# Holding back weight loads behind two joined PVs, in a one-core kernel of window attention plus gated MLP

## The chip, the cores and the metric

The kernel runs on one core of one Trainium2 chip. The metric is device time in microseconds of one execution, inputs and outputs in HBM. A core has five engines with instruction streams of their own: TensorE (PE; its weight loads are listed apart as PEld), VectorE (DVE), ScalarE (ACT), GpSimd (POOL) and SyncE (SP). They wait for each other through semaphores. Transfers are issued as instructions of an engine's stream, here nearly all of SP's, which works strictly in order: what stands behind a waiting issue waits too.

## The reference

```
xn  = layernorm(x)                                  # x: 2048 x 576, bf16
qkv = xn @ wqkv                                     # 32 heads of 18
A   = softmax(q k^T / sqrt(18), causal, window 256) v @ wo
B   = (silu(xn @ w1) * (xn @ w3)) @ w2              # 576 -> 4608 -> 576
out = x + A + B
```

## The kernel before

**Chunks.** The 2048 tokens are worked in four chunks of 512 (loop `for c in range(NC)`, line 941; chunks 0 to 3). A chunk has a projection part (q, k, v), then 36 units (line 1025), then a part called p2. In one unit 128 columns of gate and 128 of up are computed for 512 tokens: nine rounds (`for n in range(9)`, line 1033) of two matmuls that use one half of PE's rows each (`unit_pairs`, line 713), then tanh on ScalarE (722) and two multiplications on VectorE (728, 731) that leave one tile of hT. In p2 (`p2_list`, line 736) hT is multiplied by W2 (773) and the attention's output by wo (779, 699), half of the 576 output columns after the other; the residual is added (786) and the result stored (788).

**Attention between the units.** A planner counts a clock in rounds and inserts score steps (matmuls in 587, exponentials on ScalarE in 596, masks on GpSimd in 623) between rounds. Heads are grouped in four; the product of probabilities and values is a PV (644), four a chunk. PV 0 comes after a set unit (`FIRST`), PVs 1 and 2 are joined at one place (`JOINT`, line 938: unit 26 before round 6 in chunk 0, unit 27 before round 7 in chunk 1, unit 24 before round 4 in chunk 2, unit 27 before round 8 in chunk 3), PV 3 stands after unit 35. What follows a PV is spread over the next units (`later`): transposes out of PSUM (653), reciprocals (658), scaling on GpSimd (659), transposes (666), and four copies into oT issued by SP (`o_pack`, 670). For the joined PVs the first four copies are issued two units after, the other four five units after.

**Weights of gate and up.** They come in 9 column blocks a chunk, one for four units, each in six pieces of 192 KB (`load_part`, line 311). Three buffers hold blocks in turn. After every fourth unit (u = 3, 7, ... 27; line 1070) six pieces are owed, and `owe_part` issues one after rounds 3 and 8 of each following unit (line 1067), on SP, behind the matmul of that round. So the block owed after unit 23 is that of units 32 to 35, and the one owed after unit 27 is the first of the next chunk. Chunk 3 owes none after unit 27.

**W2.** Its 18 tiles a chunk (288 KB each, `load_w2`, line 342) pass through four buffers, which also hold probabilities earlier in the chunk. The first four tiles of a chunk are loaded during the units: after units 27 to 30 in chunk 0, else after units JOINT + 1, + 3, + 5 and + 7 (line 1118). In p2 each tile serves 16 matmuls, and the next tile of its buffer is loaded after them (line 777).

**The next chunk's LayerNorm.** Four tiles of 128 tokens, three of them during the units: for tile t, statistics (357 to 367) at unit JOINT - 13 + 4t, the normalizing (394) two units later, and the transposing DMA into xnT (419) three units later (`near`, line 944). Tile 3 has units 34 and 35 and a place in p2.

**Order on SP.** It is the program's order. Around the joined PVs these meet: weight pieces, transposing DMAs, W2 tiles, oT copies, and four loads of x for the residual (line 1121, after unit 29).

Of the kernel before, what the change touches and what calls it, by code (L numbers as in the profile page):

```python
# [164 lines left out]
def bass_parallel_sum__sliding_block__glu_gated_swiglu__prompt_kernel(  # L165
# [32 lines left out]
    with ExitStack() as es:  # L198
# [48 lines left out]
        def pt_keys(sl):  # L247
            kind, n = sl
            if kind in ("pt", "w2", "od"):
                return [(kind, n)]  # L250
            if kind == "sh":
                return [("sh", 2 * n), ("sh", 2 * n + 1)]
            return [("h", NF - 8 + 2 * n), ("h", NF - 7 + 2 * n)]
# [21 lines left out]
        def job():  # L275
            nonlocal job_ctr
            i = job_ctr % 3
            job_ctr += 1
            return JOBS[i]
# [14 lines left out]
        def load_x(t, eng="sp"):  # L294
            nonlocal xp_ctr
            s = xp_ctr % NXP
            xp_ctr += 1
            add(eng, lambda e: e.dma_start(xp[s][:], x2[t * 128:(t + 1) * 128, :]), w=[("xp", s)], dma=f"xp{s}")
            return s
# [638 lines left out]
        JOINT = {0: (26, 6), 1: (27, 7), 2: (24, 4), 3: (27, 8)}  # L938
        AHEAD = [40, 24, 40, 24]

        for c in range(NC):
            NS = len(steps_of(c))
            att = [(g, s) for g in range(G) for s in range(NS)]
            near = {t: tuple(JOINT[c][0] - 13 + 4 * t + k for k in (0, 2, 3)) for t in range(3)} | {3: (34, 35, 40)}
            plan = near if c + 1 < NC else {}
            stat, apply, xt = ({v[k]: i for i, v in plan.items()} for k in range(3))
            loads = {8: (2,), 17: (3,)} if c + 1 < NC else {}
# [22 lines left out]
            def later(u, what):  # L970
                side.setdefault(u, []).append(what)

            def release(j, kept):
                for g in (2 * j, 2 * j + 1):
                    for st in range(NS):
                        sl = pt_of[(c, g, st)]
                        ok = ("pt", "sh", "h", "w2") if j == 0 else ("pt", "sh")
                        if sl[0] in ok:
                            (kept if kept is not None and len(kept) < 2 and sl[0] in ("pt", "sh") else free).append(sl)
# [45 lines left out]
            for u in range(NF):  # L1025
                at_u = u
                if c == 0 and u == 0:
                    owed += 12
                if u in loads:
                    for i in loads[u]:  # L1030
                        xslot[(c + 1) * TB + i] = load_x((c + 1) * TB + i)
                b0 = jobs[u] = job()
                for n in range(9):
                    into = nxt - (clock + 9 - n)
                    if (u, n) == JOINT[c]:
                        ja = 1
                        assert next_pv == ja and ja + 1 in pv_ready and clock >= pv_ready[ja + 1], (c, next_pv, clock, pv_ready)
                        two = [job(), job()]
                        job_ctr += 1
                        kept = []  # L1040
                        _DEBUG.setdefault("joint", []).append((c, u, n, done, round(clock - pv_ready[ja + 1], 1), len([o for o in P.ops if o.eng == "pe"])))
                        for m, j in enumerate((ja, ja + 1)):
                            pv(c, j, two[m])
                            clock += PV_COST
                            release(j, kept)
                        next_pv = ja + 2
                        for m, sl in enumerate(kept):
                            uqs[2 + m:] = [pt_slot(sl).rearrange("p q r -> p (q r)").bitcast(dt.float32)]
                            uq_keys[2 + m:] = [pt_keys(sl)]
                        pv_out(two[0][0], 0)  # L1050
                        pv_out(two[0][1], 1)
                        o_scale(0)
                        pv_out(two[1][0], 2)
                        pv_out(two[1][1], 3)
                        g = 2 * ja
                        later(u, lambda g=g: (o_turn(g, 0), o_turn(g, 1), o_scale(1)))
                        later(u + 1, lambda g=g: o_turn(g + 1, 0))
                        later(u + 2, lambda g=g, ja=ja: (o_turn(g + 1, 1), o_pack(ja, "sp"), o_scale(2)))
                        later(u + 3, lambda g=g: (o_turn(g + 2, 0), o_turn(g + 2, 1), o_scale(3)))
                        later(u + 3, lambda kept=kept: free.extend(kept))  # L1060
                        later(u + 4, lambda g=g: o_turn(g + 3, 0))
                        later(u + 5, lambda g=g, ja=ja: (o_turn(g + 3, 1), o_pack(ja + 1, "sp")))
                    if (c == 0 or u or n > 1) and done < len(att) and (free or done < len(early) or done in held) and (clock >= nxt or (n == 8 and into < 3 and clock >= soon)):
                        spaced_step()
                    op = unit_pairs(c, u, n, n + 1, b0[0])
                    clock += 1
                    if n in (3, 8) or (n == 6 and c == 0 and u < 4):
                        owe_part(op)
                unit_tanh(u, b0[0])
                if u % 4 == 3 and u < NF - 8 and (c or u != 15):  # L1070
                    owed += 6
                if u == FIRST[c]:
                    j = next_pv
                    assert j == 0 and clock >= pv_ready[0], (c, clock, pv_ready)
                    next_pv += 1
                    banks = job()
                    pv(c, j, banks)
                    clock += PV_COST
                    release(j, None)
                    later(u, lambda b=banks: (pv_out(b[0], 0), pv_out(b[1], 1), o_scale(0)))  # L1080
                    later(u + 1, lambda j=j: (o_turn(2 * j, 0), o_turn(2 * j, 1), o_scale(1)))
                    later(u + 2, lambda j=j: o_turn(2 * j + 1, 0))
                    later(u + 3, lambda j=j: (o_turn(2 * j + 1, 1), o_pack(j, "sp")))
                    if j == 0:
                        for n in range(7):
                            later(u + 4 + (n if c == 0 else n // 2 + n // 6), lambda n=n: o_rest(n, "sp" if c else "act"))
                unit_h(u, b0[0])
                for what in side.pop(u, []):
                    what()
                if u in stat:  # L1090
                    t = (c + 1) * TB + stat[u]
                    for part in range(2):
                        ln_stats(t, xslot[t], part)
                if u in xt:
                    xn_send((c + 1) * TB + xt[u])
                if u in apply:
                    t = (c + 1) * TB + apply[u]
                    ln_apply(t, xslot[t])
                if c == 0 and u == 1:
                    span_main(2, G, "act", slice(2, None))  # L1100
                if c == 0 and u == 2:
                    span_last(2, G, slice(0, 1))
                if c == 0 and u in (4, 5):
                    span_last(2, G, slice(1, 3) if u == 4 else slice(3, None))
                if c == 0 and u == 13:
                    for t in range(4):
                        a0 = (4 + 14 * (t // 2)) * Dh
                        rows = A_wo[a0:a0 + 14 * Dh, :].rearrange("(s p d) f -> p s d f", p=2, d=Dh)[t % 2, :, :, :]
                        add("sp", lambda e, t=t, rows=rows: e.dma_start(wo[0:126, t, :], rows),
                            dma="wo", **{"j" if t else "w": ["wo"]})  # L1110
                if c == 0 and u == 22:
                    head = A_wo[0:4 * Dh, :]
                    add("sp", lambda e: e.dma_start(wo[126:128, 0:4, :], head.rearrange("(t d) f -> d t f", d=Dh)[16:Dh, :, :]),
                        j=["wo"], dma="wo")
                    for r in range(2):
                        add("sp", lambda e, r=r: e.dma_start(
                            wo[64 * r:64 * r + 64, 4, :], head.rearrange("(t d) f -> t d f", d=Dh)[:, 0:16, :]), j=["wo"], dma="wo")
                if u in (range(27, 31) if c == 0 else range(JOINT[c][0] + 1, JOINT[c][0] + 8, 2)):
                    load_w2(c * 2 * NFC + 4)
                if u == 29:  # L1120
                    xs = [load_x(c * TB + tt) for tt in range(TB)]
# [11 lines left out]
            for n, item in enumerate(p2_list(c)):  # L1133
# [20 lines left out]
                elif n in (100, 120) and c + 2 < NC:  # L1154
                    t = (c + 2) * TB + (n == 120)
# [32 lines left out]
```

## Time and profile before

| what | us |
|---|---|
| median of 3 runs | 558.45 |
| lowest, highest | 558.35, 559.97 |
| the profiled execution | 559.28 |
| its span (first to last instruction) | 557.5 |
| PE busy | 552.9 |
| VectorE busy | 311.2 |
| ScalarE busy | 260.3 |
| GpSimd busy | 161.9 |

The span is what the trace covers; the rest of an execution's time lies around it. All times in the views are microseconds from the span's start. In rows of groups the columns are: line, engine, operation, written and read tiles, shape and count, then busy time and mean ns of one, then idle time of the engine just before them and what ended it. In rows of a timeline: start, length, line, operation and tiles, count; neighbouring instructions of one kind are merged. In rows of DMA issues: tiles, queue, count, size of one, median time from issue to landing. In rows of waits: who waited for whom, then total, times, longest. Tiles of both weight kinds are called `w` there; L322 is a gate/up piece, L349 a W2 tile.

### The profile page before, as it was taken

To read this page: it belongs to the slowest core of one execution; us is meant where nothing else is said; L and a number is where in the kernel's file an instruction comes from. 1 tells how busy PE (TensorE), PEld (TensorE's weight loads), DVE (VectorE), ACT (ScalarE), POOL (GpSimd) and SP (SyncE) were. 2 spreads that over 40 slices of the span, in tenths; PEclk is the share of its full clock that TensorE was granted. 3 is DMA by queue.
4 is the path that set the end of the run, shared out by engine and by line. 5 is a ranking of instruction groups with operands and counts; after the bars stand their busy time and mean duration, and the time that the engine had idled before them with its cause. 6 is when DMAs were issued, how large, how long until landed. Compare 5 with 4: busy or idle time off the path is not lost.

```text
span 557.5 us, 15736 instructions
## 1 busy us (share of the span) xinstructions
PE 552.9 (99%) x6766; PEld 337.3 (60%) x6766; DVE 311.2 (56%) x581; ACT 260.3 (47%) x358; POOL 161.9 (29%) x384
## 2 busy tenths in 40 slices
PE   9999999999999999999999999999999999999998
PEld 4445454677654555477766554557776554455776
DVE  7566979610365888851046687874105577678211
ACT  6457776100387775700038787640005777755000
POOL 6314544300034453430003455423000334433000
DMA  9987996877377359566726748776582774634552
GB/s 235 224 164 181 213 191 147 173 198 187 90 144 164 112 130 185 158 178 178 198 62 139 166 107 193 147 189 148 152 188 54 137 174 109 164 106 108 159 149 65
DMA packets 127072, 85.96 MB, mean 154 GB/s; under 512 B 34179, under 2 KB 124763, under 8 KB 127003
## 3 DMA queue, kind: packets, MB, share of 16 engines
q1 hardware_dynamic: 125011, 82.69, 63.6%
q10 hardware_dynamic: 1992, 2.27, 1.7%
q8 instruction: 53, 0.87, 0.7%
q14 instruction: 16, 0.13, 0.1%
HBM read 71.29 MB, written 2.36 MB: 132 GB/s over the span
## 4 chain that ended last, share of the span: by engine, by line
PE 99%; issue 0%; DVE 0%
PE ps L713 50%; PE ps L773 25%; PE ps L461 10%; PE ps L587 6%; PE ps L644 3%; PE ps L779 3%; PE ps L808 1%; PE ps L699 0%; PE ps L406 0%; DVE ofin L786 0%; DVE oq L803 0%
## 5 line engine op out<-in xcount | busy, mean ns | idle before, releaser
L713 PE MATMUL ps<-xnT,w 64*128 64x512 bf16 x1400 | 184.9, 376 | 0.4 <-issue 0.4
L713 PE MATMUL ps<-xnS,w 64*128 64x512 bf16 x1120 | 152.4, 376 | 0.2 <-issue 0.2
L773 PE MATMUL ps<-w,hT 128*128 128x288 bf16 x1152 | 146.6, 286 | 0.0
L728 DVE SCALAR_TENSOR_TENSOR gs<-th,ps 128x512 bf16<-128x512 bf16 x144 | 97.9, 680 | 77.6 <-ACT th L722 76.9
L773 PEld LDWEIGHTS ps<-w,hT 128*128 128x128 bf16 x1152 | 112.3, 98 | 29.0 <-issue 0.4
L713 PEld LDWEIGHTS ps<-xnT,w 64*128 64x128 bf16 x1400 | 69.0, 94 | 64.7 <-issue 0.9
L722 ACT ACTIVATE th<-ps 128x512 bf16<-128x512 f32 x144 | 85.6, 594 | 40.4 <-PE ps L713 38.2
L731 DVE SCALAR_TENSOR_TENSOR hT<-gs,ps 128x512 bf16<-128x512 bf16 x144 | 98.9, 687 | 4.9
L596 ACT ACTIVATE pt<-ps 128x1024 bf16<-128x1024 f32 (+1 forms) x70 | 70.8, 1011 | 37.0 <-PE ps L587 36.7
L713 PEld LDWEIGHTS ps<-xnS,w 64*128 64x128 bf16 x1120 | 54.9, 94 | 50.3 <-issue 0.5
L786 DVE TENSOR_TENSOR ofin<-ps,xp 128x288 bf16<-128x288 f32 x32 | 13.8, 455 | 125.0 <-PE ps L779 66.9
L474 ACT ACTIVATE stage<-ps 128x512 bf16<-128x512 f32 x16 | 9.5, 596 | 142.3 <-PE ps L461 139.9
L623 POOL TENSOR_TENSOR hT<-hT,mk 128x128 int32<-128x128 int32 (+1 forms) x59 | 24.0, 429 | 175.2 <-ACT hT L596 175.2
L623 POOL TENSOR_TENSOR pt<-pt,mk 128x128 int32<-128x128 int32 (+1 forms) x124 | 50.1, 429 | 27.2 <-ACT pt L596 27.0
L587 PE MATMUL ps<-qv,kv 64*128 64x320 bf16 (+4 forms) x528 | 51.8, 260 | 0.0
L587 PEld LDWEIGHTS ps<-qv,kv 64*128 64x128 bf16 x528 | 26.2, 94 | 27.5 <-ACT hT L596 1.5
L596 ACT ACTIVATE w<-ps 128x1024 bf16<-128x1024 f32 (+1 forms) x32 | 32.3, 1010 | 12.2 <-PE ps L587 12.1
L461 PE MATMUL ps<-xnT,wp 64*128 64x512 bf16 (+1 forms) x360 | 37.9, 355 | 0.0
L596 ACT ACTIVATE hT<-ps 128x1024 bf16<-128x1024 f32 (+1 forms) x32 | 32.3, 1009 | 5.3 <-PE ps L587 4.8
L623 POOL TENSOR_TENSOR w<-w,mk 128x128 int32<-128x128 int32 (+1 forms) x56 | 22.9, 429 | 27.2 <-ACT w L596 27.1
L666 DVE STREAM_TRANSPOSE od<-oq 128x256 bf16<-128x256 bf16 x64 | 25.8, 427 | 7.0 <-POOL oq L659 7.0
L461 PEld LDWEIGHTS ps<-xnT,wp 64*128 64x128 bf16 x360 | 18.7, 94 | 14.6
(89 smaller groups left out, 381.9 us busy)
## 6 DMA issues: line engine op xcount, KB each, us to landing
w<-in_B_w_dram SPq DMA_DIRECT2D x208, 192.0 KB, 4.1
w<-in_B_w_dram SPq DMA_DIRECT2D x72, 288.0 KB, 3.4
xp<-in_A_x_dram SPq DMA_DIRECT2D x30, 144.0 KB, 3.1
out_dram<-ofin SPq DMA_DIRECT2D x32, 72.0 KB, 1.7
xnS<-xnT SPq DMA_DIRECT2D x8, 256.0 KB, 4.3
oT<-od SPq DMA_DIRECT2D x40, 36.0 KB
pt<-in_A_wqkv_dram SPq DMA_DIRECT2D x4, 288.0 KB, 6.8
hT<-in_B_w_dram SPq DMA_DIRECT2D x6, 192.0 KB, 3.6
```

What stands on the lines that cost most here:

```text
L461: op = add("pe", lambda e, out_=out_, st=st, mv=mv, n=n, r0=r0, first=first: e.matmul(out_, st, mv, start=first, stop=(part == 1 and n == ...
L587: add("pe", lambda e, r0=r0, out_=out_, kb=kb, q0=q0, nb=nb: e.matmul(out_, kb4[r0:r0 + 64, g, kb + NV - NB, :] if kb < 0 else kv[r0:r0 + ...
L596: add("act", lambda e: e.activation(pt_slot(sl)[:, 0:w, :], PS[:, SC[0]:SC[1] + 1, 0:w].rearrange("p r q -> p q r"), ACT.Exp, scale=scale) ...
L623: add("pool", lambda e, vb=vb, mm=mm: e.tensor_tensor(vb, vb, mm, ALU.mult), r=(key if n == 0 else []) + ["mk"], **{"w" if n == 0 else "j" ...
L644: add("pe", lambda e, p=p, q=q, pr=pr, sl=sl, g=g, pos=pos, q0=q0, nb=nb, col=col, first=first, n=n: e.matmul(PS[32 * q:32 * q + VW, banks ...
L666: add("dve", lambda e: e.transpose(od[i][:, g % 2, c0:c0 + CH // 2], oq[:, c0:c0 + CH // 2]), r=["oq", "oq0"], **{"j" if half or g % 2 els ...
L713: op = add("pe", lambda e, n=n, r0=r0, r=r, k=k, src=src: e.matmul(PS[:, b0 + r, :], wt[r0:r0 + 64, k, fl * 128:(fl + 1) * 128], src, star ...
L722: add("act", lambda e: e.activation(th[i][:], PS[:, bg, :], ACT.Tanh, scale=0.5), r=[("ps", bg)], w=[("th", i)])
L728: add("dve", lambda e: e.scalar_tensor_tensor(out=gs[i][:], in0=th[i][:], scalar=1.0, in1=PS[:, bg, :], op0=ALU.add, op1=ALU.mult), r=[("t ...
L731: add("dve", lambda e: e.scalar_tensor_tensor(out=hT[:, u, :], in0=gs[i][:], scalar=0.5, in1=PS[:, bu, :], op0=ALU.mult, op1=ALU.mult), r= ...
L773: add("pe", lambda e: e.matmul(bank, hT[:, f, tt * 128:(tt + 1) * 128], w2[sl][:, k, :], start=(f == 0 and half == 1), stop=False), r=[("h ...
L779: add("pe", lambda e: e.matmul(bank, oT[:, k, tt * 128:(tt + 1) * 128], wo[:, k, d0:d0 + HD], start=False, stop=(k == 3 and (half == 0 or ...
```

## The change

Three edits, all for chunks 1 to 3.

- In `quiet`, 23 rounds from the joined PVs on are marked, and no gate/up piece is issued in them: unit 27 round 7 to unit 30 round 2 in chunk 1, unit 24 round 4 to unit 26 round 8 in chunk 2, unit 27 round 8 to unit 30 round 3 in chunk 3. What was owed stays owed and goes out at the next rounds 3 and 8.
- The first four W2 tiles are loaded after units JOINT + 3, + 4, + 6 and + 7 instead of + 1, + 3, + 5 and + 7.
- The next tokens' LayerNorm tiles stand three units apart instead of four (chunks 1 and 2; chunk 3 has no next tokens), so that tile 1 comes one unit and tile 2 two units sooner. The planner leaves room for LayerNorms still to come, so two score steps of chunk 1 move one round later.

```diff
-            near = {t: tuple(JOINT[c][0] - 13 + 4 * t + k for k in (0, 2, 3)) for t in range(3)} | {3: (34, 35, 40)}
+            near = {t: tuple(JOINT[c][0] - 13 + (3 if c else 4) * t + k for k in (0, 2, 3)) for t in range(3)} | {3: (34, 35, 40)}
+            quiet = range(JOINT[c][0] * 9 + JOINT[c][1], JOINT[c][0] * 9 + JOINT[c][1] + 23) if c else ()
...
-                    if n in (3, 8) or (n == 6 and c == 0 and u < 4):
+                    if (n in (3, 8) or (n == 6 and c == 0 and u < 4)) and 9 * u + n not in quiet:
                         owe_part(op)
...
-                if u in (range(27, 31) if c == 0 else range(JOINT[c][0] + 1, JOINT[c][0] + 8, 2)):
+                if u in (range(27, 31) if c == 0 else (JOINT[c][0] + 3, JOINT[c][0] + 4, JOINT[c][0] + 6, JOINT[c][0] + 7)):
                     load_w2(c * 2 * NFC + 4)
```

On SP's stream this gives, from the joined PVs on (pieces are gate/up pieces):

| chunk | before | after |
|---|---|---|
| 1 | 2 pieces, W2 tile, 2 pieces, 4 oT, 4 x, 2 pieces, W2 tile, 4 oT, 2 W2 tiles | 4 oT, 4 x, 2 pieces, W2 tile, 2 pieces, W2 tile, 2 pieces, 4 oT, 2 W2 tiles |
| 2 | 3 pieces, W2 tile, 2 pieces, 4 oT, W2 tile, 4 pieces, 4 oT, W2 tile, 4 x, 2 pieces, W2 tile | 4 oT, 2 pieces, W2 tile, 2 pieces, W2 tile, 2 pieces, 4 oT, 4 x, 2 pieces, W2 tile, 2 pieces, W2 tile, 1 piece |
| 3 | W2 tile, 4 oT, 4 x, W2 tile, 4 oT, 2 W2 tiles | 4 oT, 4 x, 2 W2 tiles, 4 oT, 2 W2 tiles |

## The prediction

> **What bounds the kernel now.** I read the page first: busy shares, then the chain that ended last, then the costliest groups.
>
> ```profile
> span 557.5 us, 15736 instructions
> PE 552.9 (99%) x6766; PEld 337.3 (60%) x6766; DVE 311.2 (56%) x581; ACT 260.3 (47%) x358; POOL 161.9 (29%) x384
> ...
> PE 99%; issue 0%; DVE 0%
> ```
>
> TensorE (PE) is busy for 552.9 of 557.5 us and is 99% of the chain. All other engines have room. So the time is the sum of the matmuls, plus whatever makes PE wait. The waits of PE itself, in the view of waits for that engine, are these two:
>
> ```profile
> PE ps L808 <- DVE oq L803: 1.2, 1, 1.2
> PE ps L713 <- issue: 0.6, 2, 0.4
> ```
>
> The first is the start of the program. After it PE waits 0.6 us in the whole run. The change removes no matmul, so it can gain less than 1 us, unless matmuls got shorter; the group at 368.23 below keeps its full pace, 0.216 us a round, while weight pieces land. What it can lose is open-ended: a transfer that lands after its matmul is due stops PE for the difference. So the question is when each moved transfer lands. All of them go through one in-order queue, SP's. The timeline of SP from the joined PVs of chunk 2 on, columns start and length in us (a merged row runs from its first issue to the end of its last):
>
> ```profile
> 346.92 1.73 SPq L419 DMA_TRANSPOSE xnT<-xn  x1
> 349.29 6.99 SPq L322 DMA_DIRECT2D w<-in_B_w_dram  x4
> 356.32 0.61 SPq L349 DMA_DIRECT2D w<-in_B_w_dram  x1
> 356.98 1.83 SPq L322 DMA_DIRECT2D w<-in_B_w_dram  x2
> 360.27 3.14 SPq L670 DMA_DIRECT2D oT<-od  x4
> 363.46 0.47 SPq L349 DMA_DIRECT2D w<-in_B_w_dram  x1
> 363.98 2.67 SPq L322 DMA_DIRECT2D w<-in_B_w_dram  x4
> 366.76 3.09 SPq L670 DMA_DIRECT2D oT<-od  x4
> ```
>
> An issue is not free: four oT copies (L670) hold SP for 3.14 us, four weight pieces (L322) for 2.67 us, so with the gaps 0.79 and 0.68 us each, and a W2 tile (L349) takes 0.52 (363.46 to 363.98). And the oT copies wait for VectorE's transposes. In the view of SP's waits between 349.9 and 360.3 us:
>
> ```profile
> SPq L670 <- DVE rden L658: 1.6, 1, 1.6
> ```
>
> Before, SP filled the time ahead of that wait with weight pieces. That is what the change takes away.
>
> **Part by part. Pieces in chunk 2 (joined PVs in unit 24, before round 4).** Six pieces for the weights of units 32 to 35 are owed after unit 23. One goes out after round 3 of unit 24, ahead of the joined PVs. The quiet stretch is round 4 of unit 24 to round 8 of unit 26, so the other five, which went out at units 24 to 26 (rows 349.29 and 356.98: the last by 358.8 us), now go out after rounds 3 and 8 of units 27 and 28 and round 3 of unit 29. In program order they stand behind the first four oT copies, with two W2 tiles between them (now after units 27 and 28). PE reaches those rounds early enough (358 to 363 us), so SP sets the time: it idles until VectorE frees the oT copies at 360.27, is done with them at 363.46, and then issues two pieces, a W2 tile, two pieces, a W2 tile, and the fifth piece. The fifth is issued at 363.46 + 4 x 0.68 + 2 x 0.52 = 367.22 us.
>
> When is it needed? PE's timeline:
>
> ```profile
> 368.23 1.26 PE L713 MATMUL ps<-xnT,w 64*128 64x512 bf16 x10
> ...
> 376.00 0.40 PE L713 MATMUL ps<-xnT,w 64*128 64x512 bf16 x2
> ```
>
> A round is two matmuls, and ten of them in 1.26 us, the last lasting 0.40, make 0.216 us a round. The row at 376.00 is the last round of unit 35. Unit 32 begins 35 rounds earlier, at 368.44: the second round of the group at 368.23, whose first is the last of unit 31. Its matmuls need all six pieces. How long does a landing take? The view of DMA issues for 363.9 to 366.7 us:
>
> ```profile
> w<-in_B_w_dram SPq DMA_DIRECT2D x4, 192.0 KB, 4.1
> ```
>
> These four also stood right behind the oT copies, so I take their 4.1. The fifth piece lands at 371.3, and PE waits **2.9 us**. Lower end: 3.3 us, the shortest group of weight landings that I quote below, gives 2.1. Upper end: 4.8 (also below) and one long issue of 1.25 in place of 0.52 (a row of chunk 1) give 367.95 + 4.8 - 368.44 = 4.3.
>
> **W2 tiles in chunk 1 (joined PVs in unit 27, before round 7).** Here the pieces held back (four in the stretch, to round 2 of unit 30) are for chunk 2's first units and have tens of microseconds. But they are moved past: now all six go out in units 30 to 32, and three W2 tiles stand among or behind them. SP before:
>
> ```profile
> 224.03 0.61 SPq L349 DMA_DIRECT2D w<-in_B_w_dram  x1
> 225.09 1.68 SPq L322 DMA_DIRECT2D w<-in_B_w_dram  x2
> 228.60 3.15 SPq L670 DMA_DIRECT2D oT<-od  x4
> 231.79 1.89 SPq L298 DMA_DIRECT2D xp<-in_A_x_dram  x4
> 233.72 1.39 SPq L322 DMA_DIRECT2D w<-in_B_w_dram  x2
> 235.16 1.25 SPq L349 DMA_DIRECT2D w<-in_B_w_dram  x1
> 236.45 3.08 SPq L670 DMA_DIRECT2D oT<-od  x4
> 239.57 5.35 SPq L349 DMA_DIRECT2D w<-in_B_w_dram  x4
> ```
>
> Now, from 235.16 on: first W2 tile 0.52, two pieces 1.37, second tile 0.52, two pieces 1.37, which ends at 238.94; the second oT group 3.12; and the third tile at 242.06 instead of 239.57. Who needs it:
>
> ```profile
> 240.43 6.79 PE L773 MATMUL ps<-w,hT 128*128 128x288 bf16 x54
> ```
>
> W2 matmuls follow at (6.79 - 0.29) / 53 = 0.123 us, 16 to a tile, so the third tile is due at 240.43 + 32 x 0.123 = 244.36. Its landing, from the DMA views around 239.6 us and around the same place of chunk 3:
>
> ```profile
> w<-in_B_w_dram SPq DMA_DIRECT2D x2, 288.0 KB, 4.8
> w<-in_B_w_dram SPq DMA_DIRECT2D x2, 288.0 KB, 3.3
> ```
>
> With 4.8 us it lands at 246.86 (a wait of 2.5 us), with 3.3 at 245.36 (1.0). In chunk 1 transfers were queued just ahead, in chunk 3 none were; now pieces stand ahead, but the queues ran empty before them. I take the middle, 4.1: 246.16, a wait of **1.8 us**. The other tiles are covered by that wait: the first, issued at 235.16, lands by 240.0 against 240.43, and the fourth, 0.52 behind the third, is used 1.96 later.
>
> **W2 tiles in chunk 3 (unit 27).** No piece is owed there, so only the first tile moves, from 495.20 to behind the second W2 tile's place:
>
> ```profile
> 495.20 0.40 SPq L349 DMA_DIRECT2D w<-in_B_w_dram  x1
> 503.30 3.15 SPq L670 DMA_DIRECT2D oT<-od  x4
> 506.49 1.89 SPq L298 DMA_DIRECT2D xp<-in_A_x_dram  x4
> 508.42 0.43 SPq L349 DMA_DIRECT2D w<-in_B_w_dram  x1
> 510.17 2.97 SPq L670 DMA_DIRECT2D oT<-od  x4
> ```
>
> It is issued at 508.42 and lands by 513.2 even at 4.8 us; unit 35's matmuls run to beyond that, and the second tile goes out 0.5 us later, still ahead of the oT copies at 510.17. Nothing is lost; those 1.3 us of free SP are the cover, and without them the tiles would pay what chunk 1 pays.
>
> **LayerNorms.** In chunks 1 and 2 two token tiles each move one and two units earlier: per tile two statistics, an aggregate, two normalizings on VectorE, two small instructions on GpSimd, a transposing DMA on SP (1.73 us in the row at 346.92).
>
> ```profile
> L728 DVE SCALAR_TENSOR_TENSOR gs<-th,ps 128x512 bf16<-128x512 bf16 x144 | 97.9, 680 | 77.6 <-ACT th L722 76.9
> L394 DVE TENSOR_SCALAR xn<-xp,mv,rstd 128x576 bf16<-128x576 bf16 (+1 forms) x24 | 9.8, 449 | 0.0
> ```
>
> VectorE idles 77.6 us before L728, for ScalarE's tanh, and that hides them as before: three units apart, the statistics of one tile and the normalizing (0.9 us) of another still never fall into the same unit. Without that cover four times 0.9 us could show. The moved transposes hold up weight pieces by at most 1.73 us; those pieces are issued by unit 18 or 22 for units 24 or 28, five units of 1.94 us ahead, 9.7 against 4.1 + 1.73. Two score steps of chunk 1 come one round later, with nothing waiting for them. Cost: none.
>
> **Sum.** 2.9 + 1.8 = 4.7 us, PE waits that nothing overlaps, since all later work follows PE. The profiled execution took 559.28 us (span 557.5 and 1.8 around it); with the change it would take 564.0. The median of the runs is 558.45, 0.8 below the profiled one, so the median becomes **563.1 us**.
>
> The Trainium skill, "DMA: Bandwidth & Descriptors", section "Anatomy of one DMA — SWDGE (gpsimd) path", fits a DMA (of another queue type than SP's) as 2.0 us plus its bytes over 436 GB/s. As an estimate from that page a piece would land in 2.5 us and a W2 tile in 2.7, the waits would be 1.2 and 0.4, and the time 560.1; the trace's 4.1 and 3.3 to 4.8 speak against it.
>
> **Rivals.**
> *Only one wait opens.* If the third tile of chunk 1 lands as no row shows, in 2.3 us or less, that wait is gone and chunk 2's 2.1 to 2.9 stay: 560.6 to 561.4. For it: its landing has the wider bounds, 1.5 us apart. Against: the fastest row is 3.3.
> *Not slower.* With no pieces for 5 us the DMA queues are empty when the burst comes, and landings shrink. The shortest landing on the page is that of the 72 KB stores:
>
> ```profile
> out_dram<-ofin SPq DMA_DIRECT2D x32, 72.0 KB, 1.7
> ```
>
> At 1.7 us the fifth piece lands at 368.9 (0.5 late) and the tile in time: 558.9. The two waits together fall under 0.3% (1.7 us, about what a measurement of this kernel tells from no change) when landings are 2.6 us or less. Against it: 4.1 us was measured just where the queues had been let run dry by the oT wait.
> *The wait costs PE its pace.* At the start PE comes out of idleness slowly:
>
> ```profile
> 1.25 4.88 PE L808 MATMUL ps<-oq 128*128 128x512 bf16 x11 [1.25 <-DVE oq L803]
> ```
>
> Eleven matmuls of 512 columns in 4.88 us are 0.43 us each, twice the 0.216 of a round, whose two 64-row matmuls run side by side. If chunk 2's wait reached its upper 4.3 us and brought that back for 4.9 us, it would add 2.4: 558.45 + 4.3 + 1.8 + 2.4 = 567.0. The longest PE wait after the start, 0.4 us, does not show such a thing. The Trainium skill, "TensorE: Matmul & The Clock Gate", section "Part 1: The HAM clock gate (the "warmup" mystery)", says that the clock halves after a wholly idle window of about 3.4 us; by that rule 2.9 us would not trip it.
>
> **How the numbers follow.** Forecast, both waits: 0.68, own range 3.1 (2.1 + 1.0) to 6.8 (4.3 + 2.5), that is 561.5 to 565.3. One wait 0.12, not slower 0.11, lost pace 0.09. The range that leaves out about 2 in 10 takes in one wait and the spread of the runs (1.5 us above the median): 560.5 to 566.5. Slower by over 0.3%: 0.68 + 0.12 + 0.09, less 0.02 for landings between 2.6 and 3.3 us that leave little of either wait, 0.87. Within 0.3%: 0.10. Faster: 0.03, since there is under 1 us to gain.
>
> **What would show it.** In the changed trace PE should have a wait on L713 of about 2.9 us near 370 us, ended by a weight DMA, and one on L773 of about 1.8 us near 246. SP should be idle from about 350 to 360 us, then issue back to back. If PE's waits stay at 0.6 us, landings or SP's issue prices were wrong; if the pace behind a wait is 0.43, the last rival holds; if PE waits in units 24 or 28, the moved transposes were not free.

## The result and the profile after

The changed kernel is slower, and by more than forecast.

| | before | after |
|---|---|---|
| median of 6 runs, us | 559.08 | 569.3 |
| lowest, highest | 558.35, 559.97 | 566.71, 570.75 |
| ratio to before, 95% interval | | 1.0176 [1.0155, 1.0197] |
| profiled execution, its span | 559.28, 557.5 | 569.88, 568.1 |

The forecast was 563.1 us, its range 560.5 to 566.5. The sign was right; the size was not, and the time lies outside the range.

The page after, the lines that answer to those of before: span, busy time by engine, the granted clock in 40 slices, the chain that ended last.

```profile
span 568.1 us, 15736 instructions
PE 556.2 (98%) x6766; PEld 339.2 (60%) x6766; DVE 311.4 (55%) x581; ACT 260.3 (46%) x358; POOL 161.6 (28%) x384
...
PEclk9999999999999999989999999989999999999999
...
PE 94%; DMA 3%; issue 1%; DVE 1%; ACT 1%; SPq 1%
```

The work is the same instruction for instruction, yet PE is busy 3.3 us longer (556.2 against 552.9), DMA stands in the chain with 3%, and the clock row has an 8 in two slices. So two things happened: PE waited, and PE was slower for a while. The waits of PE:

```profile
PE ps L713 <- issue: 4.2, 1, 4.2
PE ps L773 <- DMA w<-in_B_w_dram: 2.7, 2, 2.5
...
PE ps L713 <- DMA w<-in_B_w_dram: 1.0, 1, 1.0
```

The first is chunk 2's unit 32, the second chunk 1's W2 tile. The third is at the program's start (near 22 us), where the change moves nothing. That the first says "issue" and not DMA is the view's inference; the piece's landing decides it. In PE's timeline (start, length) three rows behind these waits:

```profile
247.55 3.78 PE L773 MATMUL ps<-w,hT 128*128 128x288 bf16 x19 [2.52 <-DMA w<-in_B_w_dram]
...
377.36 1.04 PE L713 MATMUL ps<-xnT,w 64*128 64x512 bf16 x8 [4.23 <-issue]
...
379.85 2.18 PE L713 MATMUL ps<-xnT,w 64*128 64x512 bf16 x10
```

The last row shows the lost pace: ten matmuls in 2.18 us where before they took 1.26. Now SP's timeline, first around chunk 1's oT copies, then around chunk 2's:

```profile
228.82 3.14 SPq L670 DMA_DIRECT2D oT<-od  x4
232.00 1.89 SPq L298 DMA_DIRECT2D xp<-in_A_x_dram  x4
233.93 2.34 SPq L322 DMA_DIRECT2D w<-in_B_w_dram  x2
...
240.19 3.08 SPq L670 DMA_DIRECT2D oT<-od  x4
243.31 3.25 SPq L349 DMA_DIRECT2D w<-in_B_w_dram  x4
...
364.78 3.15 SPq L670 DMA_DIRECT2D oT<-od  x4
367.97 1.37 SPq L322 DMA_DIRECT2D w<-in_B_w_dram  x2
369.38 0.60 SPq L349 DMA_DIRECT2D w<-in_B_w_dram  x1
370.03 1.26 SPq L322 DMA_DIRECT2D w<-in_B_w_dram  x2
371.33 0.60 SPq L349 DMA_DIRECT2D w<-in_B_w_dram  x1
371.98 1.25 SPq L322 DMA_DIRECT2D w<-in_B_w_dram  x2
```

and SP's waits between 350 and 366 us:

```profile
SPq L670 <- DVE rden L658: 10.1, 1, 10.1
```

SP stood 10.1 us before the oT copies, for VectorE, with nothing issued that the weights need; then seven weight transfers went out back to back. The fifth piece left 7.20 us after the oT copies began (371.98 - 364.78). Views of DMA issues for single transfers of after (last column: us from issue to landing): the first piece of that burst, the fifth, and chunk 1's third W2 tile.

```profile
w<-in_B_w_dram SPq DMA_DIRECT2D x1, 192.0 KB, 3.4
...
w<-in_B_w_dram SPq DMA_DIRECT2D x1, 192.0 KB, 5.3
...
w<-in_B_w_dram SPq DMA_DIRECT2D x1, 288.0 KB, 4.2
```

The seven landings of the burst took 3.4, 3.8, 4.2, 4.4, 4.7, 5.1 and 5.3 us in order: each item takes longer than the one ahead, because SP issues one each 0.67 us ((371.98 - 367.97) / 6) and one lands each 0.98 (the last lands at 377.27, the first at 371.37: 5.9 / 6). The fifth piece lands at 377.27, and PE goes on at 377.36.

The granted clock is read from windows of 3.41 us laid so that the slow stretches fill one each. Columns: window, length, busy time and count of PE, PEld, DVE, ACT, POOL, then PEclk, DMA share, GB/s.

```profile
245.17:248.58 3.41, 1.03 (x9) 0.84 (x10) 1.18 (x4) 0.00 (x0) 0.67 (x1) 1.00 0.90 247
248.58:251.99 3.41, 3.41 (x16) 2.17 (x15) 0.00 (x0) 0.00 (x0) 0.00 (x0) 0.50 1.03 200
...
371.46:374.88 3.42, 1.66 (x16) 0.58 (x12) 2.42 (x4) 1.65 (x3) 0.46 (x2) 1.00 1.15 241
374.88:378.29 3.41, 0.93 (x10) 0.55 (x12) 0.33 (x1) 0.00 (x0) 0.00 (x0) 1.00 0.98 230
378.29:381.70 3.41, 3.41 (x20) 1.46 (x18) 0.52 (x1) 0.60 (x1) 0.00 (x0) 0.50 0.71 215
```

Behind each of the two waits the clock is 0.50 for exactly one such window, which costs half of it, 1.7 us. The account of the profiled execution: waits 4.2 + 2.7 + 1.0, twice 1.7 for the clock, less the 0.6 of waits that before had and after has not: 10.7 us, against 10.6 between the spans (10.2 between the medians).

### The profile page after: what moved, and what is told of

It reads as the page before. It is cut to its first block, busy times and chain, and to the rows that moved or that the text cites. A ratio compares the mean times of both kernels' runs of the same rounds, so it can differ in the third digit from the quotient of the medians.

```text
span 568.1 us, 15736 instructions
## 1 busy us (share of the span) xinstructions
PE 556.2 (98%) x6766; PEld 339.2 (60%) x6766; DVE 311.4 (55%) x581; ACT 260.3 (46%) x358; POOL 161.6 (28%) x384
## 4 chain that ended last, share of the span: by engine, by line
PE 94%; DMA 3%; issue 1%; DVE 1%; ACT 1%; SPq 1%
PE ps L713 49%; PE ps L773 25%; PE ps L461 7%; PE ps L587 6%; PE ps L644 3%; DMA w<-in_B_w_dram 3%; PE ps L779 3%; PE ps L808 1%; SPq L670 0%; PE ps L699 0%; ACT va L512 0%; ACT xnT L413 0%; DVE gs L728 0%; PE ps L406 0%; DVE hT L731 0%
## 5 line engine op out<-in xcount | busy, mean ns | idle before, releaser
L713 PE MATMUL ps<-xnT,w 64*128 64x512 bf16 x1400 | 185.5, 378 | 5.2 <-issue 4.2
L713 PE MATMUL ps<-xnS,w 64*128 64x512 bf16 x1120 | 153.1, 378 | 0.0
L773 PE MATMUL ps<-w,hT 128*128 128x288 bf16 x1152 | 148.6, 288 | 2.7 <-DMA w<-in_B_w_dram 2.7
L713 PEld LDWEIGHTS ps<-xnT,w 64*128 64x128 bf16 x1400 | 69.6, 94 | 70.4 <-issue 5.9
L713 PEld LDWEIGHTS ps<-xnS,w 64*128 64x128 bf16 x1120 | 55.3, 94 | 49.7 <-issue 0.7
```

The costliest lines, as they stand in the source:

```text
L713: op = add("pe", lambda e, n=n, r0=r0, r=r, k=k, src=src: e.matmul(PS[:, b0 + r, :], wt[r0:r0 + 64, k, fl * 128:(fl + 1) * 128], src, star ...
L773: add("pe", lambda e: e.matmul(bank, hT[:, f, tt * 128:(tt + 1) * 128], w2[sl][:, k, :], start=(f == 0 and half == 1), stop=False), r=[("h ...
```

## The experiments

Ratios are to the kernel before, run on the same chip. Theory A: held back, the pieces of chunk 2 and the tiles of chunk 1 stand behind oT copies that wait for VectorE, and go out as a burst whose last items are late. The rivals: B, the W2 places; C, the LayerNorms; D, the DMA queues cannot carry this load whatever stands ahead. Where an expectation says that the gate trips, it means that the clock halves.

**One edit at a time.** quiet_only takes the quiet stretch alone:

```diff
+            quiet = range(JOINT[c][0] * 9 + JOINT[c][1], JOINT[c][0] * 9 + JOINT[c][1] + 23) if c else ()
...
+                    if (n in (3, 8) or (n == 6 and c == 0 and u < 4)) and 9 * u + n not in quiet:
```

> Only the quiet stretch is kept; W2 tiles and LayerNorms stand as before. Theory A (pieces bunched behind the oT copies and handed to SP and the DMA queues in one burst): against the changed kernel one W2 tile fewer stands ahead of the fifth piece of chunk 2 and of the third W2 tile of chunk 1, so each wait is about 1 us shorter: about 3.2 us at unit 32 of chunk 2 and about 1.7 us in p2 of chunk 1, and each may be followed by 3.4 us at half clock (1.7 us more). Together +5 to +8.5 us, ratio 1.009 to 1.015. Rival B (the moved W2 tiles do the harm): no wait over 0.5 us, ratio 1.000 to 1.002.

w2_only takes the third edit of the change alone (W2 tiles after JOINT + 3, + 4, + 6, + 7):

> Only the W2 tiles are moved. Theory A: in chunk 1 the third tile is issued 0.5 us later than before, a wait of at most 0.6 us, no half clock; ratio 1.000 to 1.001. Rival B (the moved W2 tiles do the harm): waits of 2 us and more in chunk 1, ratio 1.005 or more.

ln_only takes the LayerNorm edit alone (three units apart):

> Only the LayerNorm tiles of chunks 1 and 2 stand three units apart. Theory A: hidden on all engines, no wait of PE, ratio 0.999 to 1.001. Rival C (the transposing DMAs, now among the pieces of units 20 to 24, push those past their units): a wait at unit 24 or 28 of chunk 1 or 2, ratio 1.003 or more.

Measured: quiet_only 565.21 against 559.55 us, 1.0097 [1.0065, 1.0129]; w2_only 559.51, 0.9996 [0.9983, 1.0008]; ln_only 559.9, 1.0008 [0.9995, 1.0021]. PE's waits in quiet_only are the same two, smaller:

```profile
PE ps L713 <- DMA w<-in_B_w_dram: 3.1, 1, 3.1
...
PE ps L773 <- DMA w<-in_B_w_dram: 0.9, 1, 0.9
```

A's forecast for quiet_only (waits of 3.2 and 1.7 us, 1.009 to 1.015) holds, but for a smaller wait in chunk 1. B and C fall as causes by themselves. But 1.0097 is about half of the whole: the W2 places cost nothing alone and some 4 us on top of the quiet stretch. In quiet_only one W2 tile of chunk 2 still goes out ahead of the oT copies; with the change both stand in the burst, ahead of the fifth piece.

**The burst without its cause.** ot_late is the changed kernel, but chunk 2's first four oT copies are issued three units later, so that the pieces stand ahead of them:

```diff
-                        later(u + 2, lambda g=g, ja=ja: (o_turn(g + 1, 1), o_pack(ja, "sp"), o_scale(2)))
+                        later(u + 2, lambda g=g, ja=ja, c=c: (o_turn(g + 1, 1), None if c == 2 else o_pack(ja, "sp"), o_scale(2)))
...
-                        later(u + 5, lambda g=g, ja=ja: (o_turn(g + 3, 1), o_pack(ja + 1, "sp")))
+                        later(u + 5, lambda g=g, ja=ja, c=c: (o_turn(g + 3, 1), o_pack(ja, "sp") if c == 2 else None, o_pack(ja + 1, "sp")))
```

> The changed kernel, but in chunk 2 the first four oT copies behind the joined PVs are issued three units later, together with the second four, so that SP does not wait for VectorE ahead of the held-back pieces. Theory A (head of the line: SP stands still behind those copies until about 365 us, then issues a burst): the five pieces go out as PE passes units 27 to 29, the fifth some 4 us sooner, and the wait of 4.2 us at unit 32 and its half clock vanish; chunk 1 keeps its wait of 2.7 us and its half clock: +4 to +5 us, ratio 1.007 to 1.009. Rival D (six pieces and two tiles in 7 us are more than the DMA queues carry, whatever stands ahead on SP): the wait at unit 32 stays above 2.5 us, ratio 1.013 or more.

Measured: 562.54 against 559.55, 1.0062 [1.0044, 1.0081]. SP's timeline and PE's waits:

```profile
365.57 1.46 SPq L322 DMA_DIRECT2D w<-in_B_w_dram  x2
367.07 6.12 SPq L670 DMA_DIRECT2D oT<-od  x8
```

```profile
PE ps L773 <- DMA w<-in_B_w_dram: 1.8, 1, 1.8
...
PE ps L713 <- issue: 0.9, 1, 0.9
```

The first row is the fifth piece, issued at 365.57, and one of the next block. Chunk 2's weight wait is gone, though not by much: the fifth piece lands at 370.2, about 0.3 us before PE begins unit 32. Chunk 1's wait, which this edit leaves, is 1.8 in this trace, with no half clock behind it (two of the eight executions show a mean clock of 0.997); the ratio is a little under the forecast 1.007 to 1.009. D falls for chunk 2: the same pieces, held just as long, cause no weight wait when no waiting issue stands ahead of them. No run moves the oT copies of chunk 1; that its tile is late for the same reason rests on SP's timeline and on quiet_only (0.9 us) against w2_only (no weight wait).

**One chunk at a time.** chunk1_only and chunk2_only make quiet stretch and W2 places in one chunk (LayerNorms as changed):

```diff
+            quiet = range(JOINT[c][0] * 9 + JOINT[c][1], JOINT[c][0] * 9 + JOINT[c][1] + 23) if c == 1 else ()
```

> Quiet stretch and moved W2 tiles in chunk 1 alone (LayerNorms as in the changed kernel). Theory A: the wait for the third W2 tile stays, 2 to 3.5 us, with 3.4 us at half clock behind it when the gate trips: +3.5 to +5 us, ratio 1.006 to 1.009, and nothing in chunk 2. If the two chunks' losses depended on each other, the parts would not add up to the whole's 1.0176.

> Quiet stretch and moved W2 tiles in chunk 2 alone. Theory A: the wait for the last piece at unit 32 stays, about 4.2 us, with 3.4 us at half clock behind it: +5.5 to +6.5 us, ratio 1.010 to 1.012, and nothing in chunk 1.

Measured: 562.62 and 567.74 against 559.82, 1.0060 [1.0038, 1.0082] and 1.0143 [1.0121, 1.0165]. PE's waits of chunk1_only, then of chunk2_only:

```profile
PE ps L773 <- DMA w<-in_B_w_dram: 2.5, 3, 1.3
PE ps L713 <- issue: 1.3, 1, 1.3
```

```profile
PE ps L713 <- issue: 6.4, 3, 4.1
```

In chunk1_only the wait for W2 tiles came in three parts, the longest 1.3 us, and the W2 matmuls behind each keep their full pace (16 in 2.13 us). The 1.3 us on L713 lies in chunk 2, in a place of which the last section speaks; so do 1.6 and 0.7 us of chunk2_only's 6.4. Chunk 2's own wait, 4.1 us, is followed by one half-clock window in the profiled execution; the other three show a mean clock of 0.994, which is two, and 1.0143 is above the forecast 1.010 to 1.012. The two parts add to 0.0203, the whole is 0.0176 with an interval to 0.0197; with the parts' own intervals they agree. Chunks 1 and 2 account for the loss, and the trace of after has no wait of PE in chunk 3.

**When does the clock halve?** Two waits of 2.5 and 4.2 us had done it; quiet_only's 3.1 us had not in its profiled execution, though the mean clock of three of its five runs is 0.997, which is one half-clock window in 563 us (1.7 / 563 = 0.3%). So the length of the wait alone does not decide. stall_a and stall_b are the kernel before with twelve made waits of PE in p2, of 1 to 5 copies on ScalarE that a W2 matmul must wait for, at different places:

```diff
+        STALL = {(0, 57): 2, (0, 121): 3, (0, 185): 4, (1, 57): 3, ...}
...
+                for _ in range(STALL.get((c, n), 0)):
+                    held_up = add("act", lambda e: e.activation(th[0][:], gs[0][:], ACT.Copy), r=[("gs", 0)], w=[("th", 0)], after=(last_pe(),))
...
+                    P.ops[made].deps.append(held_up)
```

They add only work whose result nothing uses.

> The kernel before, with twelve deliberate waits of PE in the four p2 parts, each on a chain of two, three or four ScalarE copies that starts when the matmul ahead is done; the copies write a buffer that is not in use then. Waits of about 1.3, 1.9 and 2.5 us are expected. Theory of the Trainium skill's page (the clock halves only after a window of 3.4 us that is wholly idle): no wait here reaches it, no half clock. Theory E (the window need only be mostly idle, and its grid does not move with the program: 2.4 idle of 3.4 us was enough in the changed kernel): half clock after those waits that fill some two thirds of one window of a fixed grid of 3.41 us, so after some of the longest and none of the shortest.

> As the run before, with chains of one to five copies at other places: waits of about 0.7 to 3.1 us. By the page's rule none gives half clock. By theory E about half or more of those of 2.5 to 3.1 us do, whichever lie mostly in one window of the grid, and none of those of 0.7 to 1.3 us.

Measured, one run each: 603.27 and 599.68 us, with 33.6 and 30.4 us of made waits, longer than expected (1.4 to 5.2 us each). In each trace the half-clock windows start whole multiples of 3.413 us apart (in after: 378.29 - 248.58 = 38 x 3.413), so there is a grid that stands still through a run. Six windows of stall_a on its grid, then four of stall_b:

```profile
261.99:265.41 3.42, 2.08 (x9) 1.34 (x10) 0.00 (x0) 1.25 (x2) 0.00 (x0) 0.50 0.03 6
265.41:268.82 3.41, 3.41 (x16) 2.11 (x14) 0.00 (x0) 0.00 (x0) 0.00 (x0) 0.50 0.35 87
...
555.54:558.95 3.41, 1.23 (x10) 1.00 (x11) 0.00 (x0) 1.26 (x2) 0.00 (x0) 1.00 0.38 110
558.95:562.36 3.41, 3.41 (x17) 2.17 (x15) 0.00 (x0) 0.00 (x0) 0.00 (x0) 0.50 0.37 87
...
565.78:569.19 3.41, 1.62 (x14) 1.06 (x11) 0.00 (x0) 1.69 (x3) 0.00 (x0) 1.00 0.60 167
569.19:572.60 3.41, 3.16 (x26) 2.54 (x27) 0.58 (x2) 0.20 (x1) 0.00 (x0) 1.00 0.25 67
```

```profile
112.16:115.57 3.41, 1.59 (x13) 1.29 (x14) 0.00 (x0) 0.63 (x1) 0.00 (x0) 1.00 0.50 122
115.57:118.98 3.41, 3.41 (x30) 2.73 (x28) 0.00 (x0) 0.00 (x0) 0.00 (x0) 1.00 0.60 164
...
572.95:576.36 3.41, 1.36 (x12) 0.85 (x9) 0.00 (x0) 1.92 (x4) 0.00 (x0) 1.00 0.60 165
576.36:579.77 3.41, 2.76 (x12) 1.78 (x13) 0.00 (x0) 0.60 (x1) 0.00 (x0) 0.50 0.08 8
```

Busy shares of 0.36 (1.23 / 3.41) and 0.40 are followed by half clock, 0.47 and 0.47 are not. Over after, chunk2_only, quiet_only and both stall kernels, all 13 windows with PE busy 0.40 or less were followed by one at half clock (two of the 13 were wholly idle), and of some 35 partly idle windows at full clock with 0.46 or more none was. So, from full clock, what decides is PE's idle time inside one window of the grid: over 2.0 us did, under 1.9 us did not. One window falls outside this: 261.99 of stall_a, itself at half clock and busy for 0.61, was followed by a second one at half clock, while the other half-clock windows, busy for 0.80 or more, were followed by full clock. A half clock can thus last for two windows; what decides that is not shown by a single case. A wait across a border is split: in quiet_only's profiled execution the 3.1 us lay as 1.8 and 1.3,

```profile
367.09:370.50 3.41, 1.64 (x16) 0.63 (x12) 2.45 (x4) 1.62 (x3) 0.46 (x1) 1.00 1.14 239
370.50:373.91 3.41, 2.10 (x20) 1.17 (x22) 0.30 (x1) 0.00 (x0) 0.00 (x0) 1.00 0.84 198
```

and the clock stayed at 1.00. A wait of at most 1.8 us never cost pace in these traces.

**Why the landings grew.** Of the 5.3 us, is it the queues' pace (F: one item lands each 1.0 us, so that what stands ahead counts 1.0) or SP's issue time alone (G)? pieces_first is the changed kernel with chunk 2's W2 tiles behind the pieces:

```diff
-                if u in (... (JOINT[c][0] + 3, JOINT[c][0] + 4, JOINT[c][0] + 6, JOINT[c][0] + 7)):
+                if u in (... (JOINT[c][0] + 3, JOINT[c][0] + 4, JOINT[c][0] + 6, JOINT[c][0] + 7) if c != 2 else range(29, 33)):
```

> The changed kernel, but in chunk 2 the four W2 tiles are loaded after units 29 to 32, so that none stands among the five held-back pieces. Theory F (the burst is limited by the DMA queues, which land a piece or a tile about every 1.0 us, while SP issues one in 0.65): the fifth piece lands about 2.1 us sooner and the wait at unit 32 falls from 4.2 to about 2.1 us; at that length it need not trip the gate. Theory G (SP's issues are the limit, a landing takes a fixed time after them): it falls by two issues, 1.3 us, to 2.9. Chunk 1 keeps 2 to 2.7 us. In all +4.5 to +8 us, ratio 1.008 to 1.014, lower if a gate does not trip.

Measured: 563.72 against 559.25, 1.0081 [1.0055, 1.0107].

```profile
PE ps L773 <- DMA w<-in_B_w_dram: 2.0, 2, 1.4
PE ps L713 <- DMA w<-in_B_w_dram: 1.9, 1, 1.9
```

Two items fewer ahead of the fifth piece brought its wait from 4.2 to 1.9 us, 1.15 each. It was issued 5.92 us after the oT copies began instead of 7.20, and it landed in 4.2 us instead of 5.3. F stands; by SP's price alone, 0.65 each, the landing would have kept its 5.3 and the wait would be 2.9.

**Versions that were to keep a gain.** next_last holds back only what is due late: chunk 1's six pieces for chunk 2, until after unit 32; W2 and LayerNorms as before. (The fourth W2 tile is loaded after unit 34, so in program order four of the six pieces still stand ahead of it.) next_last_ot adds the change's stretch and W2 places in chunk 2, with the oT copies of ot_late. w2_early is the kernel before with the W2 tiles after units JOINT + 1 to + 4, ahead of the second oT copies.

```diff
+            quiet = range(JOINT[c][0] * 9 + JOINT[c][1], 33 * 9) if c == 1 else ()
```

> The kernel before, with chunk 1 alone changed: its six pieces that belong to chunk 2 wait until after unit 32, and so stand behind the W2 tiles instead of among them; W2 tiles, LayerNorms and chunk 2 as before. By the theory that order decides (what is due first goes first), PE has no weight wait in chunk 1 or 2 and the third W2 tile lands with more margin than the 0.2 us it had: ratio 0.997 to 1.000. If holding pieces back is harmful by itself, a wait appears in chunk 1 as in the changed kernel, 1.003 or more.

> As the run before, and in chunk 2 the quiet stretch and W2 places of the changed kernel with the first four oT copies behind the pieces. No weight wait in either chunk: ratio 0.997 to 1.001. What the quiet stretches themselves gain or cost (PE's short waits behind the joined PVs that the profile does not explain, 0.2 to 1.6 us) is then seen alone.

> The opposite of the change: the kernel before with the first four W2 tiles of chunks 1 to 3 loaded after units JOINT + 1 to + 4, so ahead of the second four oT copies and, in part, of the x loads and the last pieces. If the margin of a transfer is set by what stands ahead of it on SP and in the DMA queues, the third W2 tile of chunk 1 lands some 4 us before it is due instead of 0.2, and executions in which it came late are gone: ratio 0.996 to 1.000. If the kernel before never lost anything there, 1.000. If the tiles now push the oT copies or pieces past their matmuls, PE waits and the ratio is over 1.002.

Measured: next_last 561.84 against 559.25, 1.0036 [1.0022, 1.0051]; next_last_ot 561.79, 1.0040 [1.0025, 1.0055]; w2_early 559.49 against 559.17, 1.0009 [0.9997, 1.0022]. Both expectations of no loss failed. SP's timeline and PE's waits in next_last:

```profile
239.07 2.69 SPq L322 DMA_DIRECT2D w<-in_B_w_dram  x4
241.81 0.60 SPq L349 DMA_DIRECT2D w<-in_B_w_dram  x1
```

```profile
PE ps L773 <- DMA w<-in_B_w_dram: 1.5, 1, 1.5
```

Four pieces came to stand right ahead of the fourth W2 tile, which landed at 248.0, after 6.2 us, and was late by 1.5 us. The pieces had tens of microseconds, the tile did not: here too they were put in front of something due sooner. Holding them until after unit 34, behind all four tiles, was not tried. next_last_ot has the same wait in chunk 1 (1.6 us) and no wait of PE in chunk 2. No version here beats the kernel before.

## Why the prediction was wrong, point by point

- **The bound: right.** PE sets the time, there was under 1 us to gain, and the loss is PE's own waiting.
- **SP's idle stretch and the burst: right.** 10.1 us for VectorE, then back to back (ot_late shows that this is the cause in chunk 2). It was placed near 350 to 360 us; it lies near 355 to 365, shifted by what chunk 1 had lost.
- **Chunk 2, the fifth piece: right place, mis-sized.** Issued 7.20 us after the oT copies began, where 367.22 - 360.27 = 6.95 was forecast, because a W2 tile held SP for 0.65 with its gap and not 0.52: 0.25 us. Landing 5.3 against 4.1: 1.2 us. The step that failed is "These four also stood right behind the oT copies, so I take their 4.1": a median of four issues was taken for the last of a burst of seven. The wait was 4.2, not 2.9. That this lies inside the stated bounds of 2.1 to 4.3 is in part luck: the landing of 5.3 is above the 4.8 of the upper end, which reached 4.3 by a long issue that did not come. The growth of the landings stood in the trace of before, between the W2 tile ahead of those four (issued at 363.46) and the last of them (366.04), in views of DMA issues for single transfers:

```profile
w<-in_B_w_dram SPq DMA_DIRECT2D x1, 288.0 KB, 3.6
...
w<-in_B_w_dram SPq DMA_DIRECT2D x1, 192.0 KB, 4.4
```

- **Chunk 1, the third W2 tile: right place, mis-sized.** Issued 14.49 us after the oT copies began (243.31 - 228.82) instead of 13.46; its first two pieces took 2.34 us where the row of before at 233.72 has 1.39 (why one of these issues was long is not shown). The landing, 4.2, was as forecast. With a wait of 0.15 us just ahead, 2.7 came instead of 1.8 and above the bound of 2.5, which varied only the landing and left the issues at their shortest row.
- **Lost pace: a rival that came true, and the largest miss.** It had a chance of 0.09 and a single place, chunk 2's wait at its upper end. It happened behind both waits, chunk 1's of 2.5 us too, 1.7 us each, 3.4 in all. The step that failed is "The longest PE wait after the start, 0.4 us, does not show such a thing": before had no wait from which to tell, and its absence was no evidence. The Trainium skill, "TensorE: Matmul & The Clock Gate", section "Part 1: The HAM clock gate (the "warmup" mystery)", whose rule is quoted beside it, puts the half clock "after ≥1 idle window (~3.4µs)", which the prediction read as wholly idle. The trace does not agree: chunk 1's window was busy for 1.03 of 3.41 us and the clock was 0.50 in the next one.
- **LayerNorms, chunk 3, score steps at nothing: right.** ln_only 1.0008; the chunks' shares leave nothing over. **W2 places:** nothing by themselves (w2_only 0.9996), but in the burst they cost the fifth piece 1.15 us each (pieces_first).
- **The other rivals: wrong.** Landings did not shrink after the queues had run empty: the first of the burst took 3.4 us, and the rest more. The fit of the Trainium skill, "DMA: Bandwidth & Descriptors", section "Anatomy of one DMA — SWDGE (gpsimd) path", which is for another queue type, gave an estimate of 2.5 us for a piece. The trace does not agree: 3.4 to 5.3 were measured.
- **The sum.** Forecast 4.7. Chunk 2 1.3 more, chunk 1 0.9 more, clock 3.4; with 1.0 at the program's start (no part of the change) and 0.6 of waits gone, that is 10.7. The forecast also stood on a median of 558.45 for before, where six runs give 559.08. The range was drawn round the waits alone: without the 3.4 us of clock, 569.3 would be 565.9, inside it.

## What to carry to other kernels

An in-order queue should not be emptied ahead of an issue that waits for another engine: what is held back then leaves behind that wait, as a burst, and the item due first must stand first in it. Price the last item of a burst by the pace at which the queue drains (here 0.98 to 1.15 us an item), not by a median landing. And when a forecast wait of PE nears 2 us, price it twice: with the wait alone and with one half-clock window (here 1.7 us) on top.

## What the hardware showed besides

How little idleness halved the clock was not expected: on a fixed grid of 3.413 us, half clock behind every full-clock window in which PE was busy for 0.40 or less, none at 0.46 or more.

The other thing is a PE wait of 0.2 to 1.6 us behind the joined PVs for which the profile shows no releaser. ln_only has the clearest in PE's timeline:

```profile
355.82 0.39 PE L713 MATMUL ps<-xnS,w 64*128 64x512 bf16 x2 [1.37 <-issue]
```

Before has 0.4 and 0.2 us of it, chunk2_only 1.6 in chunk 1 (where its pieces were not held), chunk1_only 1.3 in chunk 2 (not held either), quiet_only, w2_early and after none at all. Each begins 1.3 to 2.6 us after the start of a packet of 16 KB on the instruction queue (q8 in the page), while weight pieces fill the same DMA engines. That PE then waits for its own instructions is argued, not shown: such packets also pass without a wait (after at 352.0, w2_early at 351.5). If a quiet stretch behind the PVs removed this wait, it could win some 1.6 us at most. It did not remove it everywhere, since chunk2_only, pieces_first and ot_late have 0.7 to 0.9 us of it in chunk 2, where the pieces were held; and here the stretch and the W2 places cost 10.
